# Block 1 loaded through two DMA queues, w_in's first half in 512 KB transfers, and block 1's mask added on TensorE

## The chip, the cores and the metric

The kernel runs on one core of one Trainium2 chip. The time is device microseconds of one launch. Every kernel is run several times; the median and the range are given. A profile comes from one execution of its own, and all positions "at 24.14" are microseconds from the first instruction of that execution. A block is 512 tokens here; block 1 is the first one that the kernel works on.

## What is computed

Causal attention with a sliding window of 64, then a feed-forward layer with a squared ReLU:

```python
scores = q @ k.T / sqrt(64)                        # 8 batches, 8 heads, 576 tokens, 64 channels
scores = where((rel >= 0) & (rel < 64), scores, -1e9)   # rel = query position - key position
x = softmax(scores) @ v                            # then heads side by side: 4608 tokens x 512
h = maximum(x @ w_in, 0)                           # 512 -> 2048
out = (h * h) @ w_out                              # 2048 -> 512
```

Inputs and output are float32; the kernel computes with float16 operands.

## The kernel before

The tokens are cut into nine blocks of 512: tokens 0 to 511 of each of the eight batches, and a ninth block with the last 64 tokens of all eight. For each block the kernel runs attention for four pairs of heads, gathers the result transposed as xT, and then two matrix products: F1 (L299: 16 column tiles f of 128, each four matmuls of 512 columns that add up over four chunks c, then relu on VectorE at L310 and square on ScalarE at L311) and F2 (L335: four row tiles, 16 matmuls each). The order of all instructions on each engine is written out by hand (L367 on). From the second block on, F1 of one block, F2 of the block before and attention of the next are interleaved.

The start is another matter, as nothing is there to interleave with. Its steps, for head pairs hp = 0 to 3 of block 1 (g0):

- load_qk_pair (L140) and load_v_pair (L146) issue DMAs from SP: 256 KB for each q and k pair, two halves of 128 KB for each v pair. v comes in runs of 256 bytes, q and k in runs of 1 KB. After them load_w_in (L113) issues w_in in 16 pieces of 256 KB, piece (i, c) being 128 rows (chunk c) by 512 columns (part i). SP issues in program order. The DMAs share eight semaphore lanes, taken in turn; an issue waits for the transfer that had its lane before, so that at most eight are in flight.
- cast_qk_pair (L153) makes float16 copies, cast_v_pair (L159) and shift_v_pair (L163) two float16 arrangements of v (v_ev, and v_od shifted by 64 tokens). cast_w_in (L118) does the same for w_in. Each call names its engine.
- T (L217): eight transposes on TensorE put q and k of a pair into PSUM, and one copy takes them to SBUF.
- Sc (L229): sixteen matmuls of 64 columns for the scores, then Exp on ScalarE (L250) into the tile pm. M (L253) applies the mask on VectorE: an elementwise minimum of Exp's result with a tile that holds 65504 where a score counts and 0 where it doesn't.
- AV (L260): sixteen matmuls with v; a column of ones gives the sum. N (L275): reciprocal and multiply on VectorE. X (L286): transposes, and a copy into xT.
- F1_open (L315) runs the first three of the four chunks of F1's tiles 0 and 1, since the fourth needs pair 3's xT.
- busy (L90) runs matmuls of the identity whose result nobody reads, into a PSUM tile of their own; they stand between the real steps (24, 14, 3, 18, 12, 8, 12 and 12 of them, each 128 columns).

F1's tiles 0 to 3 need part i = 0 of w_in, tiles 4 to 7 part i = 1. After F1 of block 1 comes F2 of block 1, with w_out loaded in 16 pieces and cast on GpSimd and ScalarE, and with attention of block 2 between.

Buffers that matter: the staging pool "st" has 24 buffers of 256 KB; h2pool has two buffers that hold F1's result, of 2 MB each; the pool for pm has four; the attention accumulators at_ps are two PSUM tiles of two banks each.

Of the kernel before, what the change touches and what calls it, by code (L numbers as in the profile page):

```python
# [8 lines left out]
FP32 = mybir.dt.float32  # L9
FP16 = mybir.dt.float16  # L10
AF = mybir.ActivationFunctionType
ALU = mybir.AluOpType
# [3 lines left out]
def kernel(  # L16
# [13 lines left out]
    nc = tc.nc  # L30
# [3 lines left out]
    P = 128  # L34
    HP = H // 2
    NBLK = B + 1
    DMC = DM // P
# [24 lines left out]
    ident = const.tile([P, P], FP16, name="ident")  # L62
    mask32 = const.tile([P, 2, 64], FP32, name="mask32")
    mask = const.tile([P, 9, 64], FP16, name="mask")

    def build_constants():
        warm = const.tile([P, 1], FP32, name="warm")
        nc.vector.memset(warm[:], 0.0)
        nc.scalar.activation(out=warm[:], in_=warm[:], func=AF.Exp)
        make_identity(nc, ident[:])  # L70


        nc.gpsimd.memset(mask32[:], KEEP)
        nc.gpsimd.affine_select(
            out=mask32[:, 0, :], in_=mask32[:, 0, :], compare_op=ALU.is_ge,
            fill=0.0, base=0, pattern=[[1, 64]], channel_multiplier=-1,
        )
        nc.gpsimd.affine_select(
            out=mask32[:, 1, :], in_=mask32[:, 1, :], compare_op=ALU.is_ge,
            fill=0.0, base=-1, pattern=[[-1, 64]], channel_multiplier=1,  # L80
        )
        nc.gpsimd.affine_select(
            out=mask32[:, 1, :], in_=mask32[:, 1, :], compare_op=ALU.is_ge,
            fill=0.0, base=64, pattern=[[1, 64]], channel_multiplier=-1,
        )
        nc.vector.tensor_copy(out=mask[:, 0, :], in_=mask32[:, 0, :])
        for j in range(1, 9):
            nc.vector.tensor_copy(out=mask[:, j, :], in_=mask32[:, 1, :])

    def busy(n, pool=ps_f2, tag="f2"):  # L90

        t = pool.tile([P, 512], FP32, name="busy", tag=tag)
        for _ in range(n):
            nc.tensor.matmul(t[:, 0:P], ident[:], ident[:], start=True, stop=True)


    st = {}
# [5 lines left out]
    def copy(engine, out, in_):  # L103
        if engine is nc.scalar:
            engine.activation(out=out, in_=in_, func=AF.Copy, scale=1.0)  # L105
        else:
            engine.tensor_copy(out=out, in_=in_)  # L107
# [3 lines left out]
    w_out_sb = const.tile([P, FFC, DM], FP16, name="w_out_sb")  # L111

    def load_w_in(i):  # L113
        for c in range(DMC):
            nc.sync.dma_start(out=piece("w_in", i, c)[:],  # L115
                              in_=moe_w_in[c * P:(c + 1) * P, i * 512:(i + 1) * 512])

    def cast_w_in(i, c, engine):  # L118
        copy(engine, w_in_sb[:, c, i * 512:(i + 1) * 512], st["w_in", i, c][:])

    def load_w_out(f):
        nc.sync.dma_start(out=piece("w_out", f)[:], in_=moe_w_out[f * P:(f + 1) * P, :])
# [14 lines left out]

    def load_qk_pair(g, what, hp):  # L140
        src = {"q": q, "k": k}[what]
        nc.sync.dma_start(
            out=piece(what, g, hp)[:].rearrange("p (h x) -> p h x", h=2),
            in_=src[g, pair(hp), 0:512, :].rearrange("h (p i) d -> p h (i d)", i=4))

    def load_v_pair(g, hp):  # L146
        t = piece("v", g, hp)[:].rearrange("p (h c d) -> p h c d", h=2, c=4)
        for hh in range(2):
            nc.sync.dma_start(  # L149
                out=t[:, hh, :, :],  # L150
                in_=v[g, 2 * hp + hh, 0:512, :].rearrange("(c p) d -> p c d", p=P))

# [7 lines left out]
        copy(engine, ev[g, 0][:, :, pair(hp), 0:D].rearrange("p c h d -> p h c d"),  # L160
             st["v", g, hp][:].rearrange("p (h c d) -> p h c d", h=2, c=4))

    def shift_v_pair(g, hp, engine=None):  # L163

        t = st["v", g, hp][:].rearrange("p (h c d) -> p h c d", h=2, c=4)
        for to, of, c in ((0, 64, 0), (64, 0, 1)):
            copy(engine or nc.gpsimd,
                 od[g][to:to + 64, :, pair(hp), 0:D].rearrange("p m h d -> p h m d"),
                 t[of:of + 64, :, c:c + 3, :])
# [56 lines left out]
             tr[:].rearrange("r a (i p) -> r a p i", i=4))  # L226
        qT[g, hp, "unit"], kT[g, hp, "unit"] = qkt[:, 0, :], qkt[:, 1, :]

    def Sc(g, hp, apart=False, i=0):  # L229
        if apart:  # L230
            sc = [ps_f1.tile([P, 512], FP32, name="sc1", tag="f1") for _ in range(2)]
        else:
            both = at_ps[i]
            sc = [both[:, hh, :] for hh in range(2)]
        if (g, hp, "unit") in qT:
            qu, ku = qT[g, hp, "unit"], [kT[g, hp, "unit"]]
        else:
            qu, ku = qT[g, 0][:, hp, :], [kT[g, i][:, hp, :] for i in range(2) if (g, i) in kT]
        for j in range(8):
            kj = ku[j // 4] if g == B else ku[0]  # L240
            ks = P * (j % 4) if g == B else max(0, 64 * (j - 1))
            for hh in range(2):
                r0 = 64 * hh
                nc.tensor.matmul(sc[hh][:, j * 64:(j + 1) * 64], kj[r0:r0 + 64, ks:ks + P],  # L244
                                 qu[r0:r0 + 64, j * 64:(j + 1) * 64], start=True, stop=True)
        p = apool.tile([P, 2, 512], FP16, name="pm", tag="pm", bufs=4)
        pm[g, hp] = p
        for hh in range(2):
            if apart or hh == 0:
                nc.scalar.activation(out=p[:, hh, :] if apart else p[:], in_=sc[hh][:] if apart else both[:],  # L250
                                     func=AF.Exp, scale=1.0 / float(D) ** 0.5)
# [113 lines left out]
    PARTS[B] = ("q", "k", "k2", "v", "v2")  # L365

    with tc.manual_schedule():  # L367
        build_constants()
        g0, g1, g2, g3 = seq[:4]

        for hp in range(HP):
            load_qk_pair(g0, "q", hp)
            load_qk_pair(g0, "k", hp)
        for hp in range(HP):
            load_v_pair(g0, hp)
        for i in range(4):
            load_w_in(i)


        new_v(g0)
        for hp in range(HP):
            cast_qk_pair(g0, "q", hp, nc.vector)
            cast_qk_pair(g0, "k", hp, nc.vector)
        busy(24)
        T(g0, 0)
        busy(14)
        Sc(g0, 0)
        M(g0, 0)  # L390
        busy(3)
        T(g0, 1)
        busy(18)
        Sc(g0, 1)
        M(g0, 1)
        T(g0, 2)
        T(g0, 3, ps_f1, "f1")
        busy(12)
        Sc(g0, 2)
        for hp in range(3):  # L400
            cast_v_pair(g0, hp, nc.vector if hp == 1 else nc.gpsimd)
            shift_v_pair(g0, hp)
        Sc(g0, 3, True)
        AV(g0, 0)
        N(g0, 0)
        M(g0, 2)
        cast_v_pair(g0, 3, nc.scalar)
        shift_v_pair(g0, 3, nc.scalar)
        busy(8)
        AV(g0, 1)  # L410
        N(g0, 1)
        M(g0, 3)
        X(g0, 0)
        busy(12)
        AV(g0, 2, 0)
        N(g0, 2)
        X(g0, 1, nc.scalar, ps_f2, "f2")
        AV(g0, 3)
        N(g0, 3)
        X(g0, 2)  # L420
        busy(12, ps_f1, "f1")
        X(g0, 3, nc.scalar, ps_f2, "f2")
        for i in range(4):
            for c in range(DMC):
                cast_w_in(i, c, nc.gpsimd)
        for hp in range(2):
            load_qk_pair(g1, "q", hp)
            load_qk_pair(g1, "k", hp)
# [191 lines left out]
```

## Time and profile before

| | |
|---|---|
| median of 3 runs | 313.63 us (312.8 to 313.87) |
| the profiled execution, as timed | 313.47 us |
| its span, first to last instruction | 311.7 us |
| busy: TensorE, VectorE, ScalarE, GpSimd | 96%, 52%, 56%, 37% of the span |
| granted TensorE clock | 1.00 throughout |
| HBM read, written | 38.80 MB, 9.44 MB |
| first DMA issue | 0.81 us |
| ScalarE's first Exp of block 1 | 7.14 us |
| SP's eight v issues of block 1 | 4.90 to 12.59 us |
| SP's sixteen w_in issues | from 12.63 us |

How to read it: a busy share is the time in which an engine executes, not the time in which it does something useful at full rate; the chain of waits follows the last instruction back through whatever released it; "SPq" and "ACTq" are sequencers that issue DMAs; a bracket behind a timeline row names how long the engine stood idle before it and what ended that.

### The profile page before, as it was taken

To read this page: it belongs to the slowest core of one execution; us is meant where nothing else is said; L and a number is where in the kernel's file an instruction comes from. 1 tells how busy PE (TensorE), PEld (TensorE's weight loads), DVE (VectorE), ACT (ScalarE), POOL (GpSimd) and SP (SyncE) were. 2 spreads that over 40 slices of the span, in tenths; PEclk is the share of its full clock that TensorE was granted. 3 is DMA by queue.
4 is the path that set the end of the run, shared out by engine and by line. 5 is a ranking of instruction groups with operands and counts; after the bars stand their busy time and mean duration, and the time that the engine had idled before them with its cause. 6 is when DMAs were issued, how large, how long until landed. Compare 5 with 4: busy or idle time off the path is not lost.

```text
span 311.7 us, 6750 instructions
## 1 busy us (share of the span) xinstructions
PE 300.8 (96%) x2663; PEld 154.1 (49%) x2663; DVE 162.6 (52%) x280; ACT 174.2 (56%) x271; POOL 115.8 (37%) x209
## 2 busy tenths in 40 slices
PE   7789998999999999999999999999999999999995
PEld 6654444555445445554555455544554455444444
DVE  3667627588256737553656365636563556344300
ACT  4857746588366646744674466446644664444411
POOL 2468858973372464255346236332320000000000
PEclk9999999999999999999999999999999999999999
DMA  7999999999999999999999999999911000100023
GB/s 227 224 295 353 381 324 244 296 231 162 206 234 163 232 210 224 182 218 184 222 197 174 219 215 188 195 224 195 219 36 67 17 19 36 67 34 36 34 59 79
DMA packets 140800, 55.50 MB, mean 178 GB/s; under 512 B 125792, under 2 KB 132192, under 8 KB 140768
## 3 DMA queue, kind: packets, MB, share of 16 engines
q1 hardware_dynamic: 140608, 54.94, 83.5%
q8 instruction: 21, 0.34, 0.5%
q10 hardware_dynamic: 160, 0.13, 0.2%
q14 instruction: 11, 0.09, 0.1%
HBM read 38.80 MB, written 9.44 MB: 155 GB/s over the span
## 4 chain that ended last, share of the span: by engine, by line
PE 88%; DMA 4%; SPq 3%; DVE 2%; ACT 1%; issue 1%; POOL 0%; DVEq 0%
PE ops L339 39%; PE hps L307 38%; PE at L273 3%; PE at L244 3%; DMA st_w<-in_moe_w_in_dram 3%; PE xtr L292 2%; SPq L149 2%; DMA st_q<-in_q_dram 1%; DVE qk L107 1%; PE ops L355 1%; PE tr L223 1%; SPq L115 1%; DVE pm L257 1%; PE hps L321 0%; ACT qk L105 0%
## 5 line engine op out<-in xcount | busy, mean ns | idle before, releaser
L310 DVE TENSOR_SCALAR hr<-hps 128x512 f32<-128x512 f32 x144 | 98.7, 689 | 110.1 <-PE hps L307 108.0
L307 PE MATMUL hps<-xT,w_in_sb 128*128 128x512 f16 x564 | 138.7, 379 | 1.1 <-POOL w_in_sb L107 1.0
L311 ACT ACTIVATE h<-hr 128x512 f16<-128x512 f32 x144 | 90.4, 630 | 87.5 <-DVE hr L310 87.1
L339 PE MATMUL ops<-w_out_sb,h 128*128 128x512 f16 x560 | 136.1, 379 | 0.3 <-ACT osb L343 0.3
L339 PEld LDWEIGHTS <-h 128*128 128x128 f16 x560 | 53.1, 98 | 61.6 <-issue 0.3
L307 PEld LDWEIGHTS <-w_in_sb 128*128 128x128 f16 x564 | 52.9, 98 | 60.5 <-POOL w_in_sb L107 2.1
L107 POOL CAST v_ev<-st_v 128x512 f16<-128x512 f32 x35 | 22.1, 634 | 52.4 <-DMA st_v<-in_v_dram 52.3
L107 POOL CAST k<-st_k 128x512 f16<-128x512 f32 x36 | 23.4, 650 | 43.0 <-DMA st_k<-in_k_dram 42.7
L250 ACT ACTIVATE pm<-at 128x1024 f16<-128x1024 f32 x35 | 34.2, 1016 | 2.1 <-PE at L244 2.1
L343 ACT ACTIVATE osb<-ops 128x512 f32<-128x512 f32 x35 | 20.6, 588 | 24.9 <-PE ops L339 22.9
L257 DVE TENSOR_TENSOR pm<-pm,mask 128x1024 f16<-128x1024 f16 x36 | 26.9, 762 | 2.6 <-ACT pm L250 2.6
L283 DVE TENSOR_TENSOR xs<-at,rden 128x512 f16<-128x512 f32 x36 | 24.9, 691 | 1.2
L105 ACT ACTIVATE xT<-xtr 128x512 f16<-128x512 f16 x32 | 19.0, 594 | 7.8 <-PE xtr L292 7.8
L107 POOL CAST q<-st_q 128x512 f16<-128x512 f32 x30 | 18.5, 636 | 5.9 <-DMA st_q<-in_q_dram 4.5
L202 POOL CAST v_od<-st_v 64x512 f16<-64x512 f32 x30 | 19.0, 634 | 1.6
L273 PEld LDWEIGHTS <-pm 128*64 128x64 f16 x576 | 11.5, 110 | 8.6 <-issue 4.7
L273 PE MATMUL at<-v_ev,pm 128*64 128x65 f16 x384 | 14.4, 198 | 0.6 <-DVE xs L283 0.5
L292 PEld LDWEIGHTS <-xs 128*128 128x128 f16 x144 | 10.6, 98 | 7.6 <-DVE xs L283 0.4
L292 PE MATMUL xtr<-ident,xs 128*128 128x128 f16 x144 | 13.8, 219 | 0.3 <-DVE xs L283 0.3
L107 POOL CAST v_od<-st_v 64x384 f16<-64x384 f32 x22 | 12.4, 564 | 1.2
L105 ACT ACTIVATE qk<-tr 128x1024 f16<-128x1024 f16 x9 | 9.0, 1017 | 5.7 <-PE tr L223 3.3
L107 POOL CAST w_in_sb<-st_w 128x512 f16<-128x512 f32 x16 | 10.1, 636 | 3.3 <-DMA st_w<-in_moe_w_in_dram 2.6
(47 smaller groups left out, 117.5 us busy)
## 6 DMA issues: line engine op xcount, KB each, us to landing
st_k<-in_k_dram SPq DMA_DIRECT2D x40, 256.0 KB, 4.5
st_q<-in_q_dram SPq DMA_DIRECT2D x32, 256.0 KB, 4.6
out_dram<-osb SPq DMA_DIRECT2D x32, 256.0 KB, 3.0
st_v<-in_v_dram SPq DMA_DIRECT2D x28, 256.0 KB, 3.9
st_w<-in_moe_w_in_dram SPq DMA_DIRECT2D x16, 256.0 KB, 6.3
st_w<-in_moe_w_out_dram SPq DMA_DIRECT2D x16, 256.0 KB, 5.8
st_v<-in_v_dram SPq DMA_DIRECT2D x24, 128.0 KB, 4.8
st_q<-in_q_dram SPq DMA_DIRECT2D x8, 128.0 KB, 4.4
```

Source lines behind the costliest of these rows:

```text
L105: engine.activation(out=out, in_=in_, func=AF.Copy, scale=1.0)
L107: engine.tensor_copy(out=out, in_=in_)
L250: nc.scalar.activation(out=p[:, hh, :] if apart else p[:], in_=sc[hh][:] if apart else both[:], func=AF.Exp, scale=1.0 / float(D) ** 0.5)
L257: nc.vector.tensor_tensor(out=p[:], in0=p[:], in1=m.unsqueeze(1).broadcast_to([P, 2, 512]), op=ALU.min)
L273: nc.tensor.matmul(a[jj * 64:(jj + 1) * 64, hh, jp * VW:jp * VW + D + 1], pm[g, hp][:, hh, j * 64:(j + 1) * 64], vsel, start=True, stop=True)
L283: nc.vector.tensor_tensor(out=x[:].rearrange("p j h d -> p h j d"), in0=a[:, :, :, 0:D], in1=rden[:].unsqueeze(3).broadcast_to([P, 2, 4, D ...
L292: nc.tensor.transpose(out=tr[:, 0, jp * P:(jp + 1) * P], in_=xs[g, hp][:, jp, :, :], identity=ident[:])
L307: nc.tensor.matmul(hps[:], w_in_sb[:, c, f * P:(f + 1) * P], xT[g][:, c, :], start=(c == 0), stop=(c == DMC - 1))
L310: nc.vector.tensor_scalar(out=hr[:], in0=hps[:], scalar1=0.0, scalar2=None, op0=ALU.max)
L311: nc.scalar.activation(out=h2[g][:, f, :], in_=hr[:], func=AF.Square)
L339: nc.tensor.matmul(f2[g, ts][:], h2[g][:, f, ts * P:(ts + 1) * P], w_out_sb[:, f, :], start=(f == 0), stop=(f == FFC - 1))
L343: nc.scalar.activation(out=osb[:], in_=f2[g, ts][:], func=AF.Copy, scale=OUT_SCALE)
```

## The change

Only block 1's start is changed. q and v's first halves stay on SP's queue; k and v's second halves are issued by ScalarE, with its table load and a first tiny Exp between its second and third k. Parts 0 and 1 of w_in come in four transfers of 512 KB into one staging tile, in the pool of h2; parts 2 and 3 stay as they were. The mask of block 1 is no longer a minimum on VectorE after Exp: an identity matmul writes maskb (0 where a score counts, -65504 where not) into PSUM ahead of each score tile, and the scores are added to it. The casts and PSUM copies of block 1 go to other engines, and the order of its steps and the busy matmuls are set anew; most busy matmuls now have 512 columns. The constants are built after the DMA issues in program order, and the old mask for later blocks after block 1's attention. `dve`, `pool`, `act` are VectorE, GpSimd, ScalarE.

```diff
@@ -62,11 +62,9 @@
     ident = const.tile([P, P], FP16, name="ident")
     mask32 = const.tile([P, 2, 64], FP32, name="mask32")
     mask = const.tile([P, 9, 64], FP16, name="mask")
+    maskb = apool.tile([P, 2, 512], FP16, name="maskb", tag="pm", bufs=4)
 
     def build_constants():
-        warm = const.tile([P, 1], FP32, name="warm")
-        nc.vector.memset(warm[:], 0.0)
-        nc.scalar.activation(out=warm[:], in_=warm[:], func=AF.Exp)
         make_identity(nc, ident[:])
 
 
@@ -83,15 +81,25 @@
             out=mask32[:, 1, :], in_=mask32[:, 1, :], compare_op=ALU.is_ge,
             fill=0.0, base=64, pattern=[[1, 64]], channel_multiplier=-1,
         )
+
+        for j in range(8):
+            nc.vector.tensor_scalar(
+                out=maskb[:, 0, j * 64:(j + 1) * 64], in0=mask32[:, min(j, 1), :], scalar1=-KEEP,
+                scalar2=None, op0=ALU.add)
+
+    def build_mask():
         nc.vector.tensor_copy(out=mask[:, 0, :], in_=mask32[:, 0, :])
         for j in range(1, 9):
             nc.vector.tensor_copy(out=mask[:, j, :], in_=mask32[:, 1, :])
 
-    def busy(n, pool=ps_f2, tag="f2"):
+    def busy(n, pool=ps_f2, tag="f2", wide=True):
 
         t = pool.tile([P, 512], FP32, name="busy", tag=tag)
         for _ in range(n):
-            nc.tensor.matmul(t[:, 0:P], ident[:], ident[:], start=True, stop=True)
+            if wide:
+                nc.tensor.matmul(t[:], ident[:], maskb[:, 0, :], start=True, stop=True)
+            else:
+                nc.tensor.matmul(t[:, 0:P], ident[:], ident[:], start=True, stop=True)
 
 
     st = {}
@@ -111,12 +119,21 @@
     w_out_sb = const.tile([P, FFC, DM], FP16, name="w_out_sb")
 
     def load_w_in(i):
+        if i < 2:
+            if i == 0:
+                st["w_in"] = h2pool.tile([P, 2 * DMC, 512], FP32, name="w_st", tag="h2")
+            for c in range(0, DMC, 2):
+                nc.sync.dma_start(
+                    out=st["w_in"][:, DMC * i + c:DMC * i + c + 2, :],
+                    in_=moe_w_in[c * P:(c + 2) * P, i * 512:(i + 1) * 512].rearrange(
+                        "(c p) f -> p c f", p=P))
+            return
         for c in range(DMC):
             nc.sync.dma_start(out=piece("w_in", i, c)[:],
                               in_=moe_w_in[c * P:(c + 1) * P, i * 512:(i + 1) * 512])
 
     def cast_w_in(i, c, engine):
-        copy(engine, w_in_sb[:, c, i * 512:(i + 1) * 512], st["w_in", i, c][:])
+        copy(engine, w_in_sb[:, c, i * 512:(i + 1) * 512], st["w_in"][:, DMC * i + c, :] if i < 2 else st["w_in", i, c][:])
 
     def load_w_out(f):
         nc.sync.dma_start(out=piece("w_out", f)[:], in_=moe_w_out[f * P:(f + 1) * P, :])
@@ -137,16 +154,16 @@
 
 
 
-    def load_qk_pair(g, what, hp):
+    def load_qk_pair(g, what, hp, queue=nc.sync):
         src = {"q": q, "k": k}[what]
-        nc.sync.dma_start(
+        queue.dma_start(
             out=piece(what, g, hp)[:].rearrange("p (h x) -> p h x", h=2),
             in_=src[g, pair(hp), 0:512, :].rearrange("h (p i) d -> p h (i d)", i=4))
 
-    def load_v_pair(g, hp):
+    def load_v_pair(g, hp, queues=(nc.sync, nc.sync)):
         t = piece("v", g, hp)[:].rearrange("p (h c d) -> p h c d", h=2, c=4)
         for hh in range(2):
-            nc.sync.dma_start(
+            queues[hh].dma_start(
                 out=t[:, hh, :, :],
                 in_=v[g, 2 * hp + hh, 0:512, :].rearrange("(c p) d -> p c d", p=P))
 
@@ -160,10 +177,10 @@
         copy(engine, ev[g, 0][:, :, pair(hp), 0:D].rearrange("p c h d -> p h c d"),
              st["v", g, hp][:].rearrange("p (h c d) -> p h c d", h=2, c=4))
 
-    def shift_v_pair(g, hp, engine=None):
+    def shift_v_pair(g, hp, engine=None, parts=(0, 1)):
 
         t = st["v", g, hp][:].rearrange("p (h c d) -> p h c d", h=2, c=4)
-        for to, of, c in ((0, 64, 0), (64, 0, 1)):
+        for to, of, c in [((0, 64, 0), (64, 0, 1))[i] for i in parts]:
             copy(engine or nc.gpsimd,
                  od[g][to:to + 64, :, pair(hp), 0:D].rearrange("p m h d -> p h m d"),
                  t[of:of + 64, :, c:c + 3, :])
@@ -226,7 +243,7 @@
              tr[:].rearrange("r a (i p) -> r a p i", i=4))
         qT[g, hp, "unit"], kT[g, hp, "unit"] = qkt[:, 0, :], qkt[:, 1, :]
 
-    def Sc(g, hp, apart=False, i=0):
+    def Sc(g, hp, apart=False, i=0, add=False):
         if apart:
             sc = [ps_f1.tile([P, 512], FP32, name="sc1", tag="f1") for _ in range(2)]
         else:
@@ -236,13 +253,17 @@
             qu, ku = qT[g, hp, "unit"], [kT[g, hp, "unit"]]
         else:
             qu, ku = qT[g, 0][:, hp, :], [kT[g, i][:, hp, :] for i in range(2) if (g, i) in kT]
+        if add:
+            for hh in range(2):
+                nc.tensor.matmul(sc[hh][:], ident[:], maskb[:, 0, :], start=True, stop=False)
         for j in range(8):
             kj = ku[j // 4] if g == B else ku[0]
             ks = P * (j % 4) if g == B else max(0, 64 * (j - 1))
             for hh in range(2):
                 r0 = 64 * hh
                 nc.tensor.matmul(sc[hh][:, j * 64:(j + 1) * 64], kj[r0:r0 + 64, ks:ks + P],
-                                 qu[r0:r0 + 64, j * 64:(j + 1) * 64], start=True, stop=True)
+                                 qu[r0:r0 + 64, j * 64:(j + 1) * 64], start=not add,
+                                 stop=not add or j == 7)
         p = apool.tile([P, 2, 512], FP16, name="pm", tag="pm", bufs=4)
         pm[g, hp] = p
         for hh in range(2):
@@ -365,64 +386,77 @@
     PARTS[B] = ("q", "k", "k2", "v", "v2")
 
     with tc.manual_schedule():
-        build_constants()
         g0, g1, g2, g3 = seq[:4]
 
 
 
+
+        warm = const.tile([P, 1], FP32, name="warm")
+        nc.vector.memset(warm[:], 0.0)
         for hp in range(HP):
             load_qk_pair(g0, "q", hp)
-            load_qk_pair(g0, "k", hp)
+            load_qk_pair(g0, "k", hp, nc.scalar)
+            if hp == 1:
+                nc.scalar.activation(out=warm[:], in_=warm[:], func=AF.Exp)
         for hp in range(HP):
-            load_v_pair(g0, hp)
+            load_v_pair(g0, hp, (nc.sync, nc.scalar))
         for i in range(4):
             load_w_in(i)
+        build_constants()
 
 
         new_v(g0)
-        for hp in range(HP):
-            cast_qk_pair(g0, "q", hp, nc.vector)
-            cast_qk_pair(g0, "k", hp, nc.vector)
-        busy(24)
-        T(g0, 0)
-        busy(14)
-        Sc(g0, 0)
-        M(g0, 0)
+        dve, pool, act = nc.vector, nc.gpsimd, nc.scalar
+        busy(22, wide=False)
+        cast_qk_pair(g0, "q", 0, dve)
+        cast_qk_pair(g0, "k", 0, dve)
+        T(g0, 0, engine=dve)
+        cast_qk_pair(g0, "q", 1, pool)
+        busy(5)
+        Sc(g0, 0, add=True)
+        cast_qk_pair(g0, "k", 1, dve)
+        busy(1)
+        T(g0, 1)
+        cast_qk_pair(g0, "q", 2, dve)
+        cast_qk_pair(g0, "k", 2, pool)
         busy(3)
-        T(g0, 1)
-        busy(18)
-        Sc(g0, 1)
-        M(g0, 1)
-        T(g0, 2)
-        T(g0, 3, ps_f1, "f1")
-        busy(12)
-        Sc(g0, 2)
+        T(g0, 2, ps_f1, "f1", engine=dve)
+        busy(2)
+        Sc(g0, 1, i=1, add=True)
+        cast_qk_pair(g0, "q", 3, pool)
+        cast_qk_pair(g0, "k", 3, pool)
+        busy(2)
+        Sc(g0, 2, add=True)
+        T(g0, 3, engine=dve)
+        cast_v_pair(g0, 0, pool)
         for hp in range(3):
-            cast_v_pair(g0, hp, nc.vector if hp == 1 else nc.gpsimd)
             shift_v_pair(g0, hp)
-        Sc(g0, 3, True)
+        cast_v_pair(g0, 1, act)
+        cast_v_pair(g0, 2, act)
+        busy(5)
+        Sc(g0, 3, True, add=True)
+        cast_v_pair(g0, 3, act)
+        shift_v_pair(g0, 3, act, (1,))
+        shift_v_pair(g0, 3, pool, (0,))
         AV(g0, 0)
         N(g0, 0)
-        M(g0, 2)
-        cast_v_pair(g0, 3, nc.scalar)
-        shift_v_pair(g0, 3, nc.scalar)
-        busy(8)
-        AV(g0, 1)
+        busy(2)
+        AV(g0, 1, 0)
         N(g0, 1)
-        M(g0, 3)
         X(g0, 0)
-        busy(12)
-        AV(g0, 2, 0)
+        busy(3)
+        AV(g0, 2)
         N(g0, 2)
-        X(g0, 1, nc.scalar, ps_f2, "f2")
-        AV(g0, 3)
+        X(g0, 1, act, ps_f2, "f2")
+        AV(g0, 3, 0)
         N(g0, 3)
         X(g0, 2)
-        busy(12, ps_f1, "f1")
-        X(g0, 3, nc.scalar, ps_f2, "f2")
+        busy(2, ps_f1, "f1")
+        X(g0, 3, dve, ps_f2, "f2")
         for i in range(4):
             for c in range(DMC):
-                cast_w_in(i, c, nc.gpsimd)
+                cast_w_in(i, c, act if (i, c) == (0, 3) else pool)
+        build_mask()
         for hp in range(2):
             load_qk_pair(g1, "q", hp)
             load_qk_pair(g1, "k", hp)
```

## The prediction

> **What bounds the kernel now.** I read the whole span first, by stages (columns: us, then busy us and instruction count of TensorE, its weight loads, VectorE, ScalarE, GpSimd; granted clock; DMA share; GB/s), then the chain that ended last, then the first 36 us as a timeline.
>
> ```profile
> 6.40:16.00 9.60, 7.78 (x180) 6.49 (x178) 6.36 (x13) 7.72 (x11) 4.13 (x7) 1.00 1.03 244
> 16.00:25.00 9.00, 7.39 (x83) 4.12 (x81) 5.52 (x11) 5.46 (x10) 6.04 (x11) 1.00 0.97 308
> 25.00:36.00 11.00, 10.74 (x63) 5.12 (x61) 8.37 (x12) 8.07 (x13) 9.87 (x19) 1.00 1.05 368
> ...
> 77.00:290.00 213.00, 212.56 (x1765) 103.72 (x1764) 112.03 (x186) 117.88 (x188) 66.42 (x116) 1.00 0.84 155
> ```
>
> From 77 us on TensorE is never idle, and the diff leaves that part alone; from 25 us it is nearly full. So the time is set by when TensorE gets its unbroken stream of block 1's F1 matmuls: what moves that start moves the end. Before it the DMA engines are busy throughout (shares 0.97 to 1.05).
>
> ```profile
> 10.59 1.44 SPq L149
> 12.03 0.04 issue
> 12.08 0.51 SPq L149
> ...
> 16.02 8.12 DMA st_w<-in_moe_w_in_dram
> 24.14 0.05 issue
> 24.19 0.62 POOL w_in_sb L107
> 24.82 0.05 issue
> 24.86 7.30 PE hps L307 x33
> ```
>
> The chain (start, duration, what) says what holds that start: the eighth w_in piece (the last one of columns 512 to 1023), landing at 24.14, cast by GpSimd, then 33 matmuls without a gap (7.30/33 = 0.221 us each).
>
> ```profile
> 10.27 0.43 DVE L107 CAST k<-st_k 128x512 f16<-128x512 f32 x1 [0.39 <-DMA st_k<-in_k_dram]
> ...
> 19.39 1.46 PE L321 MATMUL hps<-xT,w_in_sb 128*128 128x512 f16 x6
> ...
> 21.55 3.03 PE L307 MATMUL hps<-xT,w_in_sb 128*128 128x512 f16 x13 [0.70 <-POOL w_in_sb L107]
> ```
>
> The timeline adds two things. Block 1's last k pair lands at about 10.25 (its cast starts at 10.27). Its attention is through at 19.39, when F1_open starts; 6 + 13 matmuls run before the stop at 24.86. Unheld, the twentieth would have come at 19.39 + 19 x 0.221 = 23.6, so w_in costs about 1.3 us. The same stream without a stop would start F1_open at 24.86 - 4.2 = **20.66**. This is the mark for the change: if w_in no longer holds TensorE, the kernel gains or loses by the distance of the new F1_open start from 20.66. With no change in w_in's landing, attention could be 1.3 us slower at no cost; with w_in earlier it could gain 1.3 us only if attention were as fast as now.
>
> **The change, part by part.** *Queues.* SP loses four k and four v issues, and has four 512 KB w_in issues for eight of 256 KB. ScalarE gets two k issues, the table load (1.28 us) and warm-up (0.20), two k, four v. Each v issue waits for the transfer eight before it on its semaphore lane: in before, SP's first v issues ran at 4.90 and 5.79, the third at 6.45, just after the second q landed. The order of the new program gives ScalarE's four v issues the waits for k pairs 0, 1, 2 and 3. **So ScalarE can't pass its fourth v issue until block 1's last k has landed**, and behind it in the same queue stands every Exp of block 1. In before ScalarE was free for the first Exp at 7.14.
>
> When that is: q and k are 2.1 MB. At the best 1 us slice of that stretch (373 GB/s) from 2.5 us on (the slice from 2 to 3 us moved half that), with the 0.5 us that the first q took beyond its 0.7 us of data (landed 3.7), k 3 would land at 2.5 + 5.6 + 0.5 = 8.6; as now, at 10.25; with one v half ahead of it in the other queue (their landings are 0.56 us apart), 10.8. I take 10.25: the DMA engines were full, and bytes are the same. The issue itself is unseen on ScalarE for v. Its two store issues at the end took 0.50 and 0.55 us, SP's eight v issues 7.69 us together, 0.5 to 1.44 each. I take 0.7, nearer to ScalarE's own rows since its queue holds half as much. ScalarE is free at T = 10.25 + 0.7 = **10.95** (ends 8.6 + 0.5 = 9.1 and 10.8 + 1.44 = 12.2).
>
> The Trainium skill ("DMA: Bandwidth & Descriptors", section "Issuing engines are not separate DMA queues") says that queues of several engines share the same 16 DMA engines and save only issue time; by that rule k 3 lands no sooner than now. The trace so far agrees, with shares near 1.0 here; a second queue running beside the first is in no row of it.
>
> *From T to F1_open*, step by step, from rows of before. First Exp, next instruction 0.92 later (9.66 to 10.58); then pair 1's copy, 1.02: T + 1.94. Scores of pair 1 0.41: 2.4. Two wide busy and two mask adds, 4 x 0.22: 3.3. Scores of pair 2 0.41: 3.7. T of pair 3 0.40: 4.1. VectorE's copy takes 1.24 (row at 35.23), while TensorE does five busy and two adds, 7 x 0.22 = 1.54: 5.6. Scores of pair 3: 6.0. AV of pair 0, 0.45: 6.45. Then VectorE's N: 0.93 for the first, 0.85 for each next (17.27 to 18.12); pair 2's waits for its AV behind X and three busy (+0.65); last N ends at 10.6. X of pair 3 and F1_open: **T + 10.85**. ScalarE's Exp 1 to 3 and v casts (1.02, 1.02, 0.63 x 3, 1.12) fit beside this: its last shift ends at T + 8.2, needed at 9.2. Now it is 19.39 with the last k at 10.25, so the new order is shorter after its start (10.85), but starts late.
>
> F1_open is at 10.95 + 10.85 = 21.8, which is 1.15 after the mark.
>
> *The mask.* Four mask steps leave VectorE (0.69 to 0.8 each); eight adds of 0.22 come to TensorE. Six of the eight lie in the sum above, the first two run while Exp waits. Building it, eight 64-column operations (0.91 for the like in before), is over by 3.3, before q lands at 3.7. The old mask's nine copies (1.1 us) move behind the last xT copy and delay the first relu by 0.2 at most; three PSUM buffers hide that. *Busy matmuls:* 103 of 128 columns become 22 of those and 25 of 512; those on the path are counted. *GpSimd* gets four q/k casts and gives up one v cast, one w_in cast and gets one shift more: about +1.7 us net, beside the 9.05 us it now waits for v. *w_in in 512 KB:* bytes the same. The last two pieces arrive together, so the last cast is ready 2 x 0.64 after landing instead of 0.67: +0.6 if w_in still held TensorE. Even with no transfer sooner than now that is 24.14 + 1.3 = 25.4, and the twentieth matmul is due at 21.8 + 4.2 = 26.0. If w_in came later by more than 0.6, it would bind again. *Later:* w_out's last cast (44.22 to 44.83) precedes its use by about 0.5 us; a later TensorE only adds to that, an earlier one needs earlier DMA too. The staging tile for w_in sits in h2's second buffer, needed again only near 57; no wait.
>
> **Sum**, on the profiled execution (313.47 us, its span 311.7; 0.16 under the median of 313.63): 313.47 + 1.15 = **314.6 us**.
>
> **Rivals.**
>
> *No real change (30%).* k 3 lands at 8.8 to 10.0 and the issue costs 0.5: T = 9.3 to 10.5, F1_open at 20.15 to 21.35, -0.5 to +0.7: 313.0 to 314.2. For it: attention's loss cancels the w_in gain. The +0.6 of paired pieces with nothing sooner gives the like, 314.1.
>
> *Faster (25%).* Two queues fill the gaps of the early transfers: the 1 us slices from 4 to 6 us moved 269 and 292 GB/s against 372 around them. The fastest end, k 3 at 8.6 and a 0.5 us issue, gives T = 9.1, F1_open at 19.95, -0.7: 312.8. My chain from T may be too long as well: it has some eight hand-overs between instructions that I count at their full length, and in the rows the next one starts 0.08 early (Exp 1.02, next after 0.92 to 0.95). That takes off 0.64: F1_open at 19.3, -1.35: **312.1**. It decides from F1_open before 19.7 and needs the eighth w_in piece cast by 19.3 + 4.2 = 23.5, so landed by 22.2, 1.9 us sooner than now. Against it: the shares near 1.0.
>
> *Slower, more strongly (inside my 45%).* The v issue is held as SP's longest, 1.44, or k 3 lands at 10.8: T = 11.7 to 12.2, F1_open at 22.55 to 23.05, +1.9 to +2.4: 315.4 to 315.9. A half-rate TensorE would come on top: 24 busy matmuls took 2.74 us at the start, 12 took 0.83 at 10.98, so a cold start costs nearly double. TensorE idles from about 10.7 to T + 2 = 12.9 while ScalarE waits; if it fell back, some 3 us of its work on the path would double in part, +1.5: 316.1. The skill ("TensorE: Matmul & The Clock Gate", section "Part 1: The HAM clock gate (the "warmup" mystery)") lets the clock fall only after an idle window of about 3.4 us; by that rule it stays, and the granted clock of 1.00 in all stages of before is no contradiction.
>
> *It doesn't do what it says:* if the v issues did not hold ScalarE, Exp 0 would run at about 8 and w_in's landing would be the limit; that is the faster case.
>
> **How the numbers follow.** Slower by over 0.3% 45%, within 0.3% 30%, faster by over 0.3% 25%; 0.3%, or 0.94 us, is about what a measurement of this kernel can tell from no change. The likeliest is 314.6, just past that bound; its own range is 314.4 to 316.0. The range for 8 in 10 goes from 312.0 (most of the faster case) to 316.0.
>
> **What would show it.** Right: ScalarE's first Exp of block 1 starts near 11, right behind its fourth v issue, which ends soon after k 3 lands; F1_open starts near 21.8; after it F1 runs with no wait on w_in. Wrong: Exp 0 before 9.5; k 3 landing before 9; a gap on GpSimd's w_in casts in F1; idle TensorE after 77 us; matmuls of F1 slower than 0.22.

## The result, and the profile after

The changed kernel takes 316.07 us (median of 10 runs, 315.44 to 317.92) against 314.03 us for the kernel before, run alongside (10 runs, 312.8 to 315.56): ratio 1.0072, 95% interval 1.0043 to 1.0101. The profiled execution took 316.14 us, 2.67 more than that of before; its span is 314.4 us. These two medians lie 2.04 us apart. Of all the executions below, one of experiment 4 took 394.95 us, at a mean granted clock of 0.757, and its ratio doesn't count it.

Stages of the changed kernel (columns as in the prediction):

```profile
6.40:16.00 9.60, 8.81 (x97) 4.42 (x95) 3.75 (x5) 4.89 (x6) 5.86 (x11) 1.00 1.22 295
16.00:25.00 9.00, 7.65 (x116) 4.14 (x116) 6.85 (x17) 4.56 (x9) 7.35 (x13) 1.00 1.05 382
25.00:36.00 11.00, 9.97 (x53) 4.78 (x53) 9.08 (x15) 7.85 (x13) 8.92 (x17) 1.00 1.06 379
77.00:290.00 213.00, 212.34 (x1796) 103.83 (x1794) 113.45 (x189) 118.02 (x189) 64.32 (x111) 1.00 0.80 150
```

From 77 us on nothing has changed. The DMA engines now move 295 and 382 GB/s in the first two stages, where before had 244 and 308. But TensorE, nearly full from 25 to 36 us in before (10.74 of 11), now lacks 1 us there, and stands still for the last 0.8 us ahead of it (from 24.18 to 26.03 in all). The chain of waits of the changed kernel says what holds it:

```profile
4.57 5.72 DMA st_v<-in_v_dram
...
10.31 1.02 ACT pm L271
...
22.06 0.29 DVE mask L91
22.35 3.03 DVE mask L93 x8
25.38 0.61 DVE hr L331
...
26.03 8.81 PE hps L328 x40
```

Two things stand in it. ScalarE's first Exp (L271) comes right behind ScalarE's four v issues, as predicted: they take from 4.57 to 10.27, the fourth from 9.89, after the last k landed at 9.87 (the chain books the stretch as a v transfer). But the last link ahead of TensorE's unbroken stream is no longer w_in, and isn't attention either: it is the nine mask copies (L91 and L93) on VectorE, with the first relu (hr, L331) behind them. The timeline of the changed kernel around that place (start, duration; in brackets the idle time before and what ended it):

```profile
21.43 1.46 PE L342 MATMUL hps<-xT,w_in_sb 128*128 128x512 f16 x6
...
21.68 3.55 POOL L115 CAST w_in_sb<-st_w 128x512 f16<-128x512 f32 x6
...
22.26 3.12 DVE L93 CAST mask<-mask 128x64 f16<-128x64 f32 x8
...
22.73 1.46 PE L328 MATMUL hps<-xT,w_in_sb 128*128 128x512 f16 x6
...
25.30 2.56 DVE L331 TENSOR_SCALAR hr<-hps 128x512 f32<-128x512 f32 x4
...
26.03 8.79 PE L328 MATMUL hps<-xT,w_in_sb 128*128 128x512 f16 x40 [1.85 <-DVE hr L331]
```

TensorE runs 6 + 6 matmuls from 21.43, fills the three PSUM buffers of F1, and then has to wait for the first relu to empty one. At 0.221 us each the thirteenth matmul was due at 21.43 + 12 x 0.221 = 24.08; it ran at 26.03. That is 1.95 us. F1_open itself lies 0.77 past the prediction's mark (21.43 - 20.66). 0.77 + 1.95 = 2.72, beside 2.67 measured. (From start to start F1's matmuls run 0.216 us apart; 0.221 has the end of the last one in it. With 0.216 the mark is 20.76 and the two terms are 0.67 and 2.01, together 2.68.)

The same copies by source line, durations in ns (least, median, most), first before, then after:

```profile
L88 DVE CAST mask<-mask x8: 183/184/195, 2.4 to 3.1; 128x64 f16<-128x64 f32 x8
```
```profile
L93 DVE CAST mask<-mask x8: 181/614/643, 22.3 to 25.2; 128x64 f16<-128x64 f32 x8
```

The same eight instructions take three times as long beside GpSimd's w_in casts. In the single instructions of the changed kernel, GpSimd's casts end at 22.298, 22.856, 23.413, 23.972, 24.590 and 25.233, and a mask copy ends 0.05 behind each of them (22.346, 22.904, 23.461, 24.019, 24.639, 25.281). Up to 24.019 no other copy ends between them; behind that one, and behind each of the last two, one more copy of 0.18 fits (24.115, 24.735, 25.379). So one or two copies go through per GpSimd cast. Not every instruction of VectorE is held like this: the relus that follow, which read PSUM, take 0.68 each beside GpSimd's casts from 25.54 and 26.23, as they do in before (0.69).

### The profile page after: what moved, and what is told of

Its sections match the earlier page's. It is cut to its first block, busy times and chain, and to the rows that moved or that the text cites. A ratio compares the mean times of both kernels' runs of the same rounds, so it can differ in the third digit from the quotient of the medians.

```text
span 314.4 us, 6652 instructions
## 1 busy us (share of the span) xinstructions
PE 302.8 (96%) x2615; PEld 151.8 (48%) x2615; DVE 165.7 (53%) x283; ACT 171.4 (55%) x269; POOL 115.1 (37%) x212
## 4 chain that ended last, share of the span: by engine, by line
PE 90%; DVE 4%; DMA 3%; ACT 1%; issue 0%; DVEq 0%
PE ops L360 39%; PE hps L328 38%; PE at L294 3%; PE at L264 3%; PE xtr L313 3%; DMA st_v<-in_v_dram 2%; DMA st_k<-in_k_dram 1%; DVE qk L115 1%; PE tr L240 1%; PE ops L376 1%; DVE mask L93 1%; PE busy L100 1%; DVE hr L331 1%; ACT qk L113 1%; PE hps L342 0%; DVE xs L304 0%
## 5 line engine op out<-in xcount | busy, mean ns | idle before, releaser
L331 DVE TENSOR_SCALAR hr<-hps 128x512 f32<-128x512 f32 x144 | 98.5, 689 | 105.6 <-PE hps L328 104.3
L115 POOL CAST k<-st_k 128x512 f16<-128x512 f32 x38 | 24.2, 637 | 48.2 <-DMA st_k<-in_k_dram 47.9
L271 ACT ACTIVATE pm<-at 128x1024 f16<-128x1024 f32 x35 | 34.1, 1015 | 8.8 <-DMA st_v<-in_v_dram 7.0
L115 POOL CAST v_ev<-st_v 128x512 f16<-128x512 f32 x34 | 21.3, 628 | 46.6 <-DMA st_v<-in_v_dram 46.6
L278 DVE TENSOR_TENSOR pm<-pm,mask 128x1024 f16<-128x1024 f16 x32 | 24.9, 793 | 2.5 <-ACT pm L271 2.5
L115 POOL CAST q<-st_q 128x512 f16<-128x512 f32 x32 | 19.7, 628 | 11.0 <-DMA st_q<-in_q_dram 9.3
L115 DVE COPY qk<-tr 128x1024 f16<-128x1024 f16 x6 | 7.3, 1225 | 13.3 <-PE tr L240 13.2
L294 PE MATMUL at<-v_ev,pm 128*64 128x65 f16 x384 | 13.7, 198 | 0.0
L294 PE MATMUL at<-v_od,pm 128*64 128x65 f16 x192 | 10.3, 194 | 0.0
```

What stands on the lines that cost most here:

```text
L278: nc.vector.tensor_tensor(out=p[:], in0=p[:], in1=m.unsqueeze(1).broadcast_to([P, 2, 512]), op=ALU.min)
L294: nc.tensor.matmul(a[jj * 64:(jj + 1) * 64, hh, jp * VW:jp * VW + D + 1], pm[g, hp][:, hh, j * 64:(j + 1) * 64], vsel, start=True, stop=True)
L331: nc.vector.tensor_scalar(out=hr[:], in0=hps[:], scalar1=0.0, scalar2=None, op0=ALU.max)
```

## The experiments

Each kernel was run 6 or 12 times beside the kernel before, and the ratio is to the runs of before made alongside. "Twentieth" is the twentieth F1 matmul, at 24.86 in before and 27.54 in the changed kernel.

**1. The mask built early.** The changed kernel with one call moved:

```diff
         build_constants()
+        build_mask()
...
             cast_w_in(i, c, act if (i, c) == (0, 3) else pool)
-        build_mask()
```

> The changed kernel with the nine copies of the old mask moved from behind block 1's last xT copy to before its first q cast. Theory (the late mask copies hold VectorE from 21.97 to 25.38, the first relus wait, TensorE stops for 1.9 us between its 12th and 13th matmul of F1): the copies take about 0.1 us apart and are over before q lands, the stop at 24.1 to 26.0 is gone, and the time falls by 1.9 us, to about the kernel before (ratio 0.998 to 1.002). F1_open stays near 21.4. Rival (the late start of F1_open is the whole of the loss, and TensorE would be held there anyway by w_in or by PSUM buffers): less than 0.5 us falls, ratio 1.005 to 1.007.

Measured: 313.71 us, ratio to before 1.001 (0.9999 to 1.002). The copies take 0.186 to 0.189 us each, at 3.1 to 3.9, and the stop is gone. The chain of this kernel:

```profile
4.76 1.03 PE tr L240 x8
...
21.63 1.29 PE hps L342 x6
22.93 7.12 PE hps L328 x33
```

F1_open runs straight into F1. This one call carries all the slowdown that can be measured. Two more things: the chain begins on TensorE, not with the v transfer (experiment 4); and F1_open at 21.47 is 0.81 past the mark, while the profiled time is only 0.31 above before's. So the mark overstates what F1_open's lateness costs by 0.5 us. 0.1 of it is the mark itself (20.76). The rest is made up later: the same relu comes 0.70 behind that of before up to 36 us, 0.56 behind from 62 to 92, and about 0.23 behind from 97 on. Why is not known.

**2. The mask in the middle,** ahead of pair 3's T, where GpSimd casts too, but not without pause:

```diff
         Sc(g0, 2, add=True)
-        T(g0, 3, engine=dve)
         cast_v_pair(g0, 0, pool)
...
+        build_mask()
+        T(g0, 3, engine=dve)
...
-        build_mask()
```

> The changed kernel with the nine mask copies on VectorE between the copies of T of pair 2 and of pair 3, where GpSimd casts v (11.9 to 15.7) and VectorE idles. Theory (each copy waits for the GpSimd cast that runs): the eight copies take about 0.3 to 0.4 us apart here too, and end 0.05 us behind GpSimd casts, about 3 us in all; pair 3's copy comes up to 0.6 us later, so the time is 0 to 0.6 us above that with the mask early. Rival (the copies are slow for another reason that belongs to their late place): 0.1 us apart here, as at the start, and the time is that of the mask early.

Measured: 313.46 us, ratio 1.0006 (0.9992 to 1.002). The nine copies take 1.65 us, not the 3 expected, nor the 1.0 of copies left alone:

```profile
L93 DVE CAST mask<-mask x8: 181/182/501, 12.8 to 14.1; 128x64 f16<-128x64 f32 x8
```

Three copies end 0.05 behind a GpSimd cast (12.845 behind 12.792, 13.464 behind 13.410, 14.080 behind 14.028), and behind each of them two more end 0.10 apart. Three GpSimd casts are stretched too, to 0.558 to 0.575 from 0.507. So the two engines do exclude each other here, but three copies go through per GpSimd cast instead of one or two. There are pauses of 0.04 to 0.06 us between GpSimd's casts here and practically none in the late place, which would explain it; but these casts are also shorter and of another shape, so the reason isn't shown.

**3. The mask late, but on ScalarE,** beside the same w_in casts:

```diff
-        nc.vector.tensor_copy(out=mask[:, 0, :], in_=mask32[:, 0, :])
+        copy(nc.scalar, mask[:, 0, :], mask32[:, 0, :])
...
-            nc.vector.tensor_copy(out=mask[:, j, :], in_=mask32[:, 1, :])
+            copy(nc.scalar, mask[:, j, :], mask32[:, 1, :])
```

> The changed kernel with the nine mask copies in their late place, but on ScalarE. Theory (only VectorE and GpSimd get in each other's way): the copies run 0.1 to 0.25 us apart beside GpSimd's casts, the first relu starts near 22.9, TensorE doesn't stop, and the time is that of the mask early, within 0.3 us. Rival (the reads of this tile, or any copy at this place, are slow on every engine): 0.4 us apart, ScalarE's first square is late by 2 us and the time gains less than 1 us.

Measured: 313.45 us, ratio 1.0000 (0.9989 to 1.0012). The copies follow each other every 0.146 us from 22.09 to 23.50, beside the same casts, and TensorE doesn't stop. So it is VectorE against GpSimd, not the place, the operand or the data.

**4. v back on SP alone,** on top of experiment 1, so that ScalarE has no v issue ahead of its Exp:

```diff
-            load_v_pair(g0, hp, (nc.sync, nc.scalar))
+            load_v_pair(g0, hp)
```

> Mask early, and all eight v issues of block 1 on SP's queue, so that ScalarE issues only the four k. Theory (ScalarE's first Exp waits for the last k through the fourth v issue): the first Exp starts at about 8.8, when its scores are there, not at 10.31; F1_open moves 1.5 us forward to about 19.9; w_in still lands near 20.5 for its eighth piece, due as cast by 24.1, so the time falls by 1.5 us against the mask early, about 0.4% under the kernel before. Rival (w_in lands sooner only because v comes through two queues): the eighth piece lands near 24 again, its cast is ready at 25.4, TensorE waits for it and the time is that of the mask early or up to 0.5 us above.

Measured: 313.41 us, ratio 1.0002 (0.9987 to 1.0017). The first Exp comes at 9.37, not 8.8, and F1_open at 21.63, not 19.9. The chain of this kernel names TensorE:

```profile
5.80 2.13 PE busy L100 x5
7.93 0.85 PE at L258 x2
8.79 0.54 PE at L264 x12
```

The five busy matmuls of 512 columns ahead of the first scores take 0.43 us each, the two mask adds behind them too: twice the 0.221 of F1's. With ScalarE free, TensorE at half rate holds the first Exp nearly as long. The 8.8 was read off the changed kernel, where the half rate ended at 8.0 and the first scores were through at 8.73; in the execution of this experiment the half rate lasted until 10.4. My theory that ScalarE's issues are what block 1 pays for fell in this form.

**5. Fewer busy matmuls at the cold start,** on top of experiment 4 (twelve wide ones less before the first three scores):

```diff
-        busy(5)
+        busy(1)
         Sc(g0, 0, add=True)
...
-        busy(1)
         T(g0, 1)
...
-        busy(3)
         T(g0, 2, ps_f1, "f1", engine=dve)
-        busy(2)
         Sc(g0, 1, i=1, add=True)
...
-        busy(2)
         Sc(g0, 2, add=True)
```

> The kernel with the mask early and all v issues on SP, with twelve of the wide busy matmuls before pair 2's scores taken out (five become one before the first scores, the one, three, two and two after them go). In the run before it ScalarE was free at 3.4 but the first Exp started at 9.37, because TensorE ran five busy matmuls of 0.43 us each and two mask adds, at half rate, in front of the first scores. Theory (TensorE's queue of cold busy matmuls holds what ScalarE's issues held before): the first Exp starts at about 7.7, F1_open at 18.9 to 19.7, w_in's part 1 is cast by 21.9 and due after 22.9, so the time falls by 1.9 to 2.7 us against the mask early: 311.0 to 311.8, ratio 0.992 to 0.995 to the kernel before. Rival (the busy matmuls are what brings TensorE to full rate): the scores and transposes of all four pairs run at half rate, the clock comes up 2 us later or more, and the time is within 0.7 us of the mask early. Rival (w_in holds): TensorE waits for GpSimd's cast of w_in in F1.

Measured: 311.34 us, ratio 0.9926 (0.9906 to 0.9946); the profiled execution 311.08 us, its first Exp at 7.71, F1_open at 18.70, twentieth at 22.80. Its chain:

```profile
5.74 0.43 PE busy L100
6.17 0.85 PE at L258 x2
...
18.86 1.29 PE hps L342 x6
20.16 9.94 PE hps L328 x46
```

The half rate stays (until about 9.7), but less is done in it. This is faster than both kernels, by 2.3 us and more.

**6. The same cut, with v's second halves left on ScalarE:** experiment 5 without experiment 4's edit.

```diff
+            load_v_pair(g0, hp, (nc.sync, nc.scalar))
-            load_v_pair(g0, hp)
```

> The same with the second v halves issued by ScalarE again, as in the change; the mask stays early. Theory (ScalarE's issues, waiting for k pairs, set the first Exp as soon as TensorE's busy matmuls don't): the fourth v issue ends at 9.6 to 10.3, the first Exp starts right behind it, F1_open comes at 20.2 to 20.9, and the time is 1 to 2 us above the run with v on SP. Rival (these issues never mattered, only TensorE's queue): the same time as with v on SP, within 0.4 us.

Measured: 314.21 us (312.65 to 314.47; the profiled one, at 312.83, is among the shortest), ratio 1.0005 (0.9986 to 1.0025). Its chain:

```profile
2.38 6.80 DMA st_k<-in_k_dram
...
9.20 0.37 ACTq L166
...
9.62 1.02 ACT pm L271
```

This is the predicted chain, step by step: the last k lands at 9.18, ScalarE's fourth v issue takes 0.37, and the first Exp follows at 9.62, 1.91 later than in experiment 5. F1_open is 1.60 later (20.30). ScalarE's four issues cost 1.75 us by the two profiled executions (312.83 - 311.08), 0.8% by the ratios (1.0005 / 0.9926), once TensorE doesn't cover them. The medians lie 2.87 us apart, as eight of experiment 6's twelve executions took 313.94 to 314.47 and only four 312.65 to 312.93; no trace shows one of the eight.

**7. 512 KB transfers alone,** in the kernel before:

```diff
+        if i < 2:
+            if i == 0:
+                st["w_in"] = h2pool.tile([P, 2 * DMC, 512], FP32, name="w_st", tag="h2")
+            for c in range(0, DMC, 2):
+                nc.sync.dma_start(
...
+            return
```

> The kernel before with w_in's first half in four 512 KB transfers, and nothing else of the change. If the size of the transfers is what brought w_in's eighth piece from 24.14 to 20.52: it lands near 20.5 here, TensorE has no stop after F1_open, and the time is 1.0 to 1.3 us under the kernel before (ratio 0.996). If the second queue is: it lands at 24 and is cast 0.6 us later than before, ratio 1.000 to 1.002.

Measured: 313.19 us, ratio 0.9982 (0.9966 to 0.9998). The second half of part 1 lands at 23.77 (24.14 before); the twentieth comes 1.29 behind it (0.72 before), since two casts follow the landing, at 25.06. In time the size brings next to nothing.

**8. Two queues alone,** in the kernel before:

```diff
-            load_qk_pair(g0, "k", hp)
+            load_qk_pair(g0, "k", hp, nc.scalar)
...
-            load_v_pair(g0, hp)
+            load_v_pair(g0, hp, (nc.sync, nc.scalar))
```

> The kernel before with k and the second v halves issued by ScalarE, and nothing else of the change; w_in stays in 256 KB pieces. Theory (ScalarE's queue stands behind the last k): the copy of pair 0's T, the first thing for ScalarE, starts behind the fourth v issue at 9.6 to 10.3 and not at 5.6, the first Exp near 11.5 and not at 7.14, F1_open near 22; the time is 1 to 2 us above the kernel before. If the second queue is what brings w_in sooner, its eighth piece lands near 20.5; if not, near 24. Rival (block 1's attention has that much room): no change in time.

Measured: 316.5 us, ratio 1.0092 (1.0073 to 1.011). w_in's eighth piece lands at 20.54, as early as in the changed kernel (20.52) and 3.6 before the 24.14 of before. SP, with half the v issues and no k, comes to its first w_in issue at 10.06 instead of 12.63. But ScalarE comes to its first copy only at 9.94, the first Exp at 11.67, F1_open at 24.67. And something comes on top. First the timeline of TensorE in this kernel, then its stages of 2 us (granted clock third from the end):

```profile
11.02 0.61 PE L244 MATMUL at<-qk 64*128 64x64 f16 x16 [4.08 <-ACT qk L105]
```
```profile
10.00:12.00 2.00, 0.98 (x21) 0.89 (x22) 0.00 (x0) 1.30 (x2) 1.21 (x3) 0.51 1.39 218
12.00:14.00 2.00, 2.00 (x22) 2.00 (x21) 0.79 (x1) 1.72 (x2) 1.83 (x4) 0.50 1.22 277
14.00:16.00 2.00, 2.00 (x31) 1.71 (x30) 0.00 (x0) 0.58 (x1) 1.83 (x4) 0.50 1.11 382
```

TensorE stands idle for 4.08 us, and the granted clock falls to half until past 16 us (0.78 from 16 to 18). The changed kernel avoids this: its busy matmuls and transposes run while ScalarE waits, and its longest pause there is 0.79 us, at a clock of 1.00. The Trainium skill ("TensorE: Matmul & The Clock Gate", section "Part 1: The HAM clock gate (the "warmup" mystery)") lets the clock fall after an idle window of about 3.4 us; both kernels agree with it.

**9. Only k on ScalarE,** in the kernel before: experiment 8 without its v edit.

```diff
-            load_qk_pair(g0, "k", hp)
+            load_qk_pair(g0, "k", hp, nc.scalar)
```

> The kernel before with block 1's four k issues on ScalarE, behind its table load, and nothing else; all v stays on SP, so nothing on ScalarE waits for a transfer. Theory (the second queue is what brings w_in sooner, and ScalarE is blocked only by issues that wait): w_in's eighth piece lands near 20.6 as in the runs with k on ScalarE, not at 24.1; the first Exp comes at 7.1 to 8.5, k 0 being issued 1.5 us later; F1_open at 19.4 to 20.2 and TensorE doesn't stop behind it: 0.5 to 1.3 us under the kernel before, ratio 0.996 to 0.998. Rival (w_in comes sooner only when v is spread over both queues): it lands near 24, ratio 1.000 to 1.003.

Measured: 313.0 us, ratio 0.9986 (0.997 to 1.0003). The eighth piece lands at 22.60, between 24.14 and 20.54, where 20.6 was expected; SP's first w_in issue comes at 10.66. F1 has no stop (F1_open 19.30, twentieth 23.40). The profiled execution took 312.41 us, 1.06 less than that of before, but the interval reaches past 1.

**10. Still fewer busy matmuls,** on top of experiment 5:

```diff
-        busy(5)
+        busy(3)
         Sc(g0, 3, True, add=True)
...
-        busy(3)
         AV(g0, 2)
```

> The fastest kernel so far (mask early, v on SP, twelve busy matmuls out) with five more out: five before pair 3's scores become three, and the three before pair 2's AV go. Theory (they lie on the path: 0.2 us beyond VectorE's copy, and 0.6 us ahead of pair 2's AV): F1_open moves from 18.7 to about 17.9, and w_in's eighth piece, cast by 22.0, is due at 22.0: 0.5 to 0.8 us faster than that kernel, ratio 0.990 to 0.992 to the kernel before. Rival (w_in is the bound now): TensorE stops for a w_in cast in F1, the time is within 0.3 us of that kernel.

Measured: 310.94 us, ratio 0.9916 (0.9893 to 0.9939). F1_open comes at 18.62, not 17.9, 0.08 before that of experiment 5. The new bound, in this kernel's chain:

```profile
10.53 5.10 DMA st_v<-in_v_dram
...
15.71 0.63 ACT v_ev L113
...
16.92 0.60 ACT xT L113
...
17.57 0.38 PE xtr L313 x4
```

The last v pair lands at 15.63; its cast and shift on ScalarE stand ahead of an xT copy that TensorE waits for. In experiment 5 that pair landed at 13.84, so this bound may belong to this one execution.

**11. 256 KB pieces again,** on top of experiment 5: load_w_in and cast_w_in as in the kernel before.

```diff
-        if i < 2:
-            if i == 0:
-                st["w_in"] = h2pool.tile([P, 2 * DMC, 512], FP32, name="w_st", tag="h2")
...
-            return
```

> The fastest kernel so far with w_in's first half back in eight 256 KB pieces in the staging pool. Theory (the size of the transfers does nothing, the queues do): the eighth piece lands near 20.6, F1_open stays at 18.7, the time is that of the kernel with 512 KB within 0.3 us. Rival (the size counts): w_in's pieces land 1 us later or more, TensorE waits in F1, the time is 0.5 us above or more.

Measured: 310.95 us, ratio 0.9919 (0.9896 to 0.9941); the eighth piece at 20.66, F1_open at 19.12, twentieth at 23.22. The size of the transfers decides nothing here either.

Experiments 5, 10 and 11 can't be told apart by their intervals; each is 0.7 to 0.8% faster than before.

## Why the prediction was right or wrong

The sign was right and the size was not: 1.15 us forecast, 2.67 by the profiles, 2.04 by the medians, and the median of 316.07 lies 0.07 above the range. That the sign was right is luck: the lateness that was forecast costs 0.2% at most (experiment 1), and the slowdown comes from a term that the prediction put at nothing.

*ScalarE free at T = 10.95:* the mechanism is right, the time 0.64 too late. k 3 landed at 9.87 (10.25 taken), the issue took 0.37 (0.7 taken), and the first Exp started at 10.31, right behind it.

*From T to F1_open 10.85:* right within 0.3. It took 11.1 (10.31 to 21.43). Its terms hold, but the reason behind the start was only half the truth: experiment 4 takes the v issues off ScalarE and wins nothing, because TensorE at half rate holds the first Exp too (0.43 us for each of five busy matmuls and two adds). I had counted the cold start only as a risk after an idle stretch. ScalarE's price shows once that cover is gone: 1.75 us by the profiles, experiment 6 against 5.

*F1_open at 21.8, 1.15 past the mark:* 21.43, 0.77 past it. By itself that comes out close to no change: experiment 1, with everything but the late mask copies, is at 1.001. This was the rival with 30%.

***The mask's nine copies: "1.1 us ... delay the first relu by 0.2 at most; three PSUM buffers hide that".*** This step failed. Its 1.1 us was the time of copies with no cast of GpSimd beside them; beside GpSimd's casts they took from 21.97 to 25.38, 3.4 us. The cover can be worked out: the thirteenth matmul was due at 24.08, the relu in front of it takes 0.61, so the copies could run until about 23.4, 1.4 us from 21.97. Copies of 1.1 us would have fitted; at 3.4 they are 2.0 too long, and 1.95 is what TensorE lost. The missing question was what GpSimd does at that moment: in the program order the copies stand right behind sixteen w_in casts, fifteen of them on GpSimd. Before's own profile held a hint: another VectorE instruction on SBUF, the mask's minimum (L257), took 0.68 us where no GpSimd cast ran beside it (at 10.61 and 73.78), and 1.09 where a cast had begun just ahead of it:

```profile
14.73 0.61 POOL L107 CAST v_ev<-st_v 128x512 f16<-128x512 f32 x1
...
14.80 1.09 DVE L257 TENSOR_TENSOR pm<-pm,mask 128x1024 f16<-128x1024 f16 x1
```

The Trainium skill ("SBUF — State Buffer", section "Who interferes with whom") says that a cast on VectorE can take the port pair it shares with GpSimd, and that the later of the two waits for the other's whole instruction while ScalarE waits for nobody. Experiments 1 and 3 agree with it. How high the price is depends on the place: 1.65 us for the same nine copies in experiment 2.

*w_in lands no sooner than now:* wrong, though without effect, as attention was later in any case. Here is what the DMA engines moved in each 1 us slice from 0 to 40 us, before and then after:

```profile
GB/s 0 4 183 372 269 292 373 343 329 249 213 216 80 224 238 225 240 313 141 246 324 387 395 408 315 356 365 312 357 368 365 374 393 383 387 391 356 375 385 381
```
```profile
GB/s 0 12 188 367 383 331 353 352 295 223 217 219 228 310 385 389 383 381 389 393 387 381 399 360 363 350 353 376 386 383 387 383 387 389 387 387 389 373 357 350
```

From 14 to 21 us it is 381 to 393 where before had 141 to 324, although before's mean DMA share was near 1.0: a full share did not mean full bandwidth. The Trainium skill has a rule that queues of several engines save only issue time ("DMA: Bandwidth & Descriptors", section "Issuing engines are not separate DMA queues"). It covers a part of the measurement: with the second queue alone (experiment 8), SP's first w_in issue comes 2.57 us sooner, and the eighth piece lands 3.60 sooner. It doesn't give the last 1.0 us, nor the rate: from 14 to 21 us, 247 GB/s on average in before, 354 in experiment 8 and 387 in the changed kernel. Why is open. 512 KB transfers alone raise the rate to 299 and the landing hardly (experiment 7), and beside k on ScalarE the eighth piece lands as early in 256 KB pieces (20.66 in experiment 11) and with all of v on SP (20.66 in experiments 4 and 11). k alone brought 1.5 us in the kernel before (9), less than the 1.97 by which its first w_in issue came sooner.

*+0.6 for the paired pieces:* right where it can be seen, 1.29 against 0.72 in experiment 7. *TensorE's clock stays:* right; a pause of 0.79 us left the rate as it was, and so did one of 1.47 in experiment 6. *Rivals:* the v issues do hold ScalarE, so the change does what it says. The faster rival's gaps did fill (383 and 331 GB/s from 4 to 6 us, for 269 and 292) and the eighth piece landed early enough for it (20.52), but F1_open was nowhere near 19.7. Of the slower rival's mechanisms none occurred, its size came from the mask.

## What to carry to other kernels

When small instructions of VectorE are moved, look up what GpSimd runs at their new place, and, if they read and write SBUF, price them by GpSimd's instructions there, not by their own duration; ScalarE or a place without GpSimd's casts cost nothing of the kind here. A step that is "hidden" needs its cover as a number (here 1.4 us) to be compared with its worst duration. Matmuls that keep TensorE busy cost path time while it still runs at half rate, and an issue on a compute engine that waits for a transfer holds all compute behind it: each can hide the other, so take both away before judging one.

## What the runs showed of the hardware

- VectorE's casts from float32 to float16 in SBUF and GpSimd's exclude each other. Beside casts practically without pause, VectorE's 64-column copies went from 0.10 to 0.39 us apart (nine in 3.4 us); copies on ScalarE beside the same casts weren't held (0.146 us apart), nor were VectorE's relus, which read PSUM (0.68).
- After the start TensorE ran at half rate until 6.2 us in before, until 8.0 in the changed kernel's execution, and until 10.1 and 10.4 in those of experiments 1 and 4, with nearly the same TensorE instructions up to there as the changed kernel, though matmuls had been running since 1.42 with one pause of 0.8. Why it differs is open. The granted clock read 1.00 all that time, while 512 columns took 0.43 us. It shows a fall (experiment 8: 0.51), but did not show the start.
- A second queue alone raised the mean rate between 14 and 21 us from 247 to 354 GB/s, and w_in's eighth piece landed 3.6 us sooner, while SP's first w_in issue came 2.57 us sooner. The cause of the rest was not found.
